# A third residual tile, nine exponential rooms, two banks by turns for the values' sums, and ten pairs of heads a tile in the first FFN blocks

## The chip, the core and the metric

The kernel runs on one core of a Trainium2 chip. The core has a matrix engine (TensorE, PE in the profile, with its weight loads as PEld), a vector engine (VectorE, DVE), an engine for functions (ScalarE, ACT), a general engine (GpSimd, POOL) and a queue that issues transfers (SyncE, SP). Each runs its own instructions in the order of the program and waits for the others by semaphores. Matrix products land in PSUM, eight banks of 128 x 512 numbers of four bytes; all else lies in the on-chip memory SBUF. The metric is the device time of one execution in microseconds (us), lower is better.

## What is computed

One transformer layer on 2048 tokens of 576 features, everything in 32-bit floats: layer norm, attention of 32 query heads of 18 features over one shared key and value head, a residual, a second layer norm, and a bilinear FFN with 4608 hidden features and a residual.

```python
def _A_ref(x, wq, wk, wv, wo):
    q = (x @ wq).reshape(B, S, H, Dh).transpose(0, 2, 1, 3)
    k, v = x @ wk, x @ wv
    scores = jnp.einsum("bhqd,bkd->bhqk", q, k) * (Dh ** -0.5)
    p = _softmax(scores, axis=-1)
    o = jnp.einsum("bhqk,bkd->bhqd", p, v)
    return o.transpose(0, 2, 1, 3).reshape(B, S, H * Dh) @ wo
...
h = x + _A_ref(_layernorm(x), A_wq, A_wk, A_wv, A_wo)
g, u = _layernorm(h) @ w_gate, _layernorm(h) @ w_up
return h + (g * u) @ w_down
```

## The kernel before

**Blocks, groups and pairs.** The tokens fall into four blocks of 512 queries. Attention of a block is eight groups of four heads; a group goes over sixteen stretches of 128 keys, and for each stretch there are two pairs of heads. So `pair` (line 576) is called 256 times a block, 1024 times in all, in one fixed order counted by `n_pair`. One call issues the scores: two products that run at the same time in two halves of the array, into a PSUM room of two banks (`ps_s`, two rooms), and one exponential on ScalarE of 128 x 1024 numbers from that room into an SBUF room P (`p_tile`, line 566; six rooms at first, seven from the 240th pair). The pair is half of a stretch (`half`); when the second is issued the stretch is put into `pend`. `flush(n)` (line 604) takes the n oldest stretches of `pend` and issues their values: eight matrix instructions for each stretch, which sum P times V over the keys of a group in one PSUM bank (`ps_a`), the four heads in four strips of 32 columns. At a group's last stretch DVE turns the sum (`os`, line 612), and the rest of the group's work is put into the list `aux`: dividing by the row sums (`normalise`), every two groups splitting a chunk of heads in a high and a low part (`chunk`), multiplying it with the output weights and adding to the residual (`project`), and after the fifth chunk the statistics of the second layer norm. `run_aux` (line 621) takes one or two due entries at a time.

**The FFN.** `ffn(b)` (line 970) goes over 36 tiles of 128 hidden features for the 512 tokens of block b. A tile has 27 steps j, nine pieces of the features times three combinations of high and low parts; a step is two products side by side, one for the gate (`pg`) and one for the up half (`pu`). While there are pairs of the blocks up to b + 2 left (`on`), the tile issues a pair before steps 0, 4, 8, 12, 16, 20, 24 and one behind the copy of the gate: eight, except in the last tile of a block but the fourth, which issues none. Then ScalarE copies `pg` (`g`, line 1020), DVE multiplies `pu` with it into the hidden tile (`hf`, line 1024), and all stretches in `pend` are flushed. Without pairs left, `pg` and `pu` share one of the rooms that the scores had (`gu`). Hidden tiles come in couples, an even and an odd one. Their sums and splits (`left_first` in the odd tile, `left`, `left_sums` in the next even tile behind step 8, a cast of 128 x 1024 numbers on ScalarE) make the left side of a down product, which `down` (line 896) issues at the end of the next even tile: fourteen stages of three products of 128 x 288 in three banks, two of `ps_f` and one of `ps_m`. After a stage the partial sum is added to the residual, either by DVE or by a copy on ScalarE (`tmp`, a ring of five) and an addition on POOL. A stage that returns to a bank waits for the reader of the stage before it.

**PSUM.** Two rooms of two banks for scores, two banks `f` (for `pg`, `pu`, y), one bank `m` (y, and small products), one bank `a` (the values' sum): eight in all.

**Weights and residuals.** `load_w` (line 850) brings the FFN weights of a tile (576 KB) into one of two rooms `wr`; `split_w`, behind step 3, splits the next tile's weights on POOL and DVE into one of two rooms `ws` and then asks for the load two tiles ahead. `split_wo_0` (line 722) splits the five pieces of the first block's output weights; three rooms `wo_r` hold them as they come, and a fourth and a fifth piece are asked for behind the splits of the second and third. The residual of a block is a tile `h` of 512 tokens; there are two. The third block's is loaded at the end of `ffn(0)` (line 1041), into the room that the first block's output leaves, the fourth's at the end of `ffn(1)`. `project` of a block runs only when its residual is there (`b in self.h`, line 681).

**Order.** `run` (line 1160) first does keys, values and queries beside the first pairs, then `blocks` (line 1120), which finishes attention of the first block, and then the four `ffn`. The program order on every engine is written out by these calls.

Of the kernel before, what the change touches and what calls it, by code (L numbers as in the profile page):

```python
# [25 lines left out]
P = 128  # L26
# [28 lines left out]
class Block:  # L55
# [20 lines left out]
    def ps_m(self, name):  # L76
        return self.ps.tile([P, TB], F32, tag="m", bufs=1, name=name)
# [4 lines left out]
    def ps_a(self, name):  # L82
        return self.ps.tile([P, TB], F32, tag="a", bufs=1, name=name)
# [520 lines left out]
    def flush(self, n):  # L604

        for b, g, t, Ps in self.pend[:n]:
            if t == 0:
                self.acc = self.ps_a(f"acc{b}_{g}")
            self.values(self.acc, Ps, t)
            if t == NT - 1:  # L610
                os_ = self.os[g] = self.op.tile([P, TB], F32, tag="os", bufs=1, name=f"os{b}_{g}")
                self.dve.transpose(os_, self.acc)
                if b == 0 and g == NG - 1:
                    self.normalise(b, g, os_)
                else:
                    self.aux.insert(len(self.aux) if b else 0, (self.round + 1, lambda b=b, g=g, o=os_: self.normalise(b, g, o), None))
        del self.pend[:n]
# [80 lines left out]
    def chunk_of(self, b, c):  # L698
        to = self.heads_to(b, c)
        (self.split_tail if b and c == 4 else self.split)(*to, self.ob[0:rows(b, c), c])  # L700

# [15 lines left out]
    def load_wo_0(self, c):  # L717

        r = self.wo_r0[c] = self.w0.tile([P, D], F32, tag="wo_r", bufs=3, name=f"wo_r{c}")
        self.sp.dma_start(r, self.wo0[:, c])  # L720

    def split_wo_0(self):

        self.wo_0 = self.wp.tile([P, 2, 5, D], F32R, tag="X", bufs=1, name="wo_0")
        for c in range(3):
# [124 lines left out]
    def load_w(self, n):  # L850

        if n < NF * NB:
            r = self.wr[n] = self.wp.tile([P, 9, P], F32, tag="wr", bufs=2, name=f"wr{n}")
            self.sp.dma_start(r, self.wgu[n % NF])

    def split_w(self, n):
        if n < NF * NB:
# [3 lines left out]
            self.load_w(n + 2)  # L861
# [34 lines left out]
    def down(self, b, pair):  # L896
# [4 lines left out]
        if pair == NC - 1:  # L901
# [13 lines left out]
            def add(s, n):  # L915
                hs, y = h[:, s, n * HD:(n + 1) * HD], ys.pop((s, n))[:, :HD]
                if b < NB - 1 and n:
                    z = self.tmp[:, self.n_tmp % 5]
# [27 lines left out]
        for i, (t, bank, (x, w), first, (s, n), on_dve) in enumerate(STAGES):  # L946
# [7 lines left out]
            else:  # L954
                z = self.tmp[:, self.n_tmp % 5]
# [5 lines left out]
    def room(self):  # L961
# [5 lines left out]
        self.tmp = self.hh.tile([P, 5, HD], F32, tag="tmp", bufs=1, name="tmp")  # L967
        self.n_tmp = 0

    def ffn(self, b):  # L970
        pe, act, dve = self.pe, self.act, self.dve
        X, hid, todo = self.X, [], None
        for f in range(NF):
# [56 lines left out]
            if todo and on:  # L1030
                drain(self.down(b, *todo))
                self.more_wd(b, 7)
# [12 lines left out]
    def load_x(self, b):  # L1045
        h = self.h[b] = self.hp.tile([P, NQ, D], F32, tag="h", name=f"h{b}")
# [64 lines left out]
    def begin(self, first):  # L1111
# [6 lines left out]
        self.p_next, self.wo_r0, self.wo_in, self.yos, self.n_yo, self.due, self.odd = -1, {}, set(), [], 0, 0.0, 0  # L1118

    def blocks(self):  # L1120
# [4 lines left out]
        self.load_w(1)  # L1125
# [28 lines left out]
        else:  # L1154
            self.load_wd(WD_BUFS)
        for b in range(NB):
# [3 lines left out]
    def run(self):  # L1160
# [6 lines left out]
        self.tqs, self.p2 = [], None  # L1167
        self.begin(True)
        with ExitStack() as st:
# [3 lines left out]
            self.ps, self.w0 = pool("ps", 1, space=PSUM), pool("w0", 3)  # L1173
# [7 lines left out]
            with tc.tile_pool(name="p0q", bufs=1) as self.p0q:  # L1181
# [4 lines left out]
                with tc.tile_pool(name="qb", bufs=2) as self.qb:  # L1186
# [7 lines left out]
                    while live:  # L1194
                        if self.n_pair >= WO_FROM and not self.wo_r0:
                            for c in range(3):
# [10 lines left out]
            self.wp, self.hh, self.p2 = pool("w", 2), pool("hid", 4), pool("P2", 1)  # L1207
# [17 lines left out]
P2_FROM = 240  # L1225
# [126 lines left out]
```

## Time and profile before

| what | us |
|---|---|
| median of three runs | 2287.75 |
| lowest and highest run | 2286.09, 2287.89 |
| profiled execution, first to last instruction (span) | 2285.5 |
| mean of one exponential (1024 of them) | 1.027 |
| mean of one copy of y (408) | 0.400 |
| mean of one cast of the sums S (68) | 1.043 |
| mean of one multiplication hf (96 with pairs) | 0.691 |

The profile tells the span of the profiled execution, from its first to its last instruction; it gives no other time for it. The span lies 0.6 us below the lowest of the runs. In the chain of waits a row is a start in us, a duration in us, an engine with what it writes and the line, and how often. In a timeline the duration is that of the merged instructions from the first start to the last end; the brackets give the idle time of the engine before them and what ended it. In a group of instructions the numbers behind the bar are the busy time in us, the mean of one in ns, and the idle time before them in us with what ended most of it. PEld is the loading of weights into the matrix engine, which may run beside its products.

### The profile page before, as it was taken

The numbers are of one execution on the slowest core, as the hardware profiler recorded it, in microseconds if no ns is written. First come the engines' busy times: TensorE is split into PE (matmuls) and PEld (weight loads), VectorE is DVE, ScalarE is ACT, GpSimd is POOL, SyncE is SP. The second block draws the span as 40 slices with busy tenths as digits, with TensorE's granted clock in tenths as the row PEclk, the third lists the DMA queues.
The fourth block names the chain that finished last, engine by engine and source line by source line (L and its number), as shares of the span: only waits on it lengthen the run. The fifth ranks groups of instructions, "written<-read, shape, count | busy, mean of one in ns | idle before, by whom it ended". The sixth has DMA issues, their size and how long they took to land.

```text
span 2285.5 us, 45923 instructions
## 1 busy us (share of the span) xinstructions
PE 2264.4 (99%) x18114; PEld 1610.0 (70%) x18114; DVE 1183.9 (52%) x2152; ACT 1438.0 (63%) x1877; POOL 683.1 (30%) x856
## 2 busy tenths in 40 slices
PE   8999999999999999999999999999999999999998
PEld 6433345677777667677767777777767788898887
DVE  8332435565656566343434455444444476566565
ACT  5899887777676676767666767667677623232332
POOL 4000002455554444122221222222122233333332
PEclk9999999999999999999999999999999999999999
DMA  5222314444333444633333443643333355655553
GB/s 174 75 79 72 117 30 136 144 143 147 134 123 129 141 159 135 210 114 123 113 113 108 126 129 125 193 126 120 100 120 116 122 172 174 212 172 172 179 185 112
DMA packets 127129, 306.75 MB, mean 134 GB/s; under 512 B 17553, under 2 KB 17681, under 8 KB 126265
## 3 DMA queue, kind: packets, MB, share of 16 engines
q1 hardware_dynamic: 126905, 303.73, 40.6%
q8 instruction: 145, 2.38, 0.4%
q14 instruction: 79, 0.65, 0.1%
HBM read 233.76 MB, written 55.67 MB: 127 GB/s over the span
## 4 chain that ended last, share of the span: by engine, by line
PE 95%; DVE 2%; DMA 1%; ACT 1%; issue 0%; SPq 0%; POOL 0%; DVEq 0%; ACTq 0%; POOLq 0%
PE pg L990 21%; PE acc L601 20%; PE y L950 17%; PE gu L990 13%; PE s L596 12%; PE pu L990 5%; PE yo L754 3%; PE psq L448 2%; PE y L908 1%; DMA X<-X 1%; PE psk L236 0%; DVE XT L89 0%; PE ye L908 0%; DVE bsa L103 0%; ACT P L597 0%
## 5 line engine op out<-in xcount | busy, mean ns | idle before, releaser
L597 ACT ACTIVATE P<-s 128x1024 f32<-128x1024 f32 x1024 | 1025.4, 1027 | 263.6 <-PE s L596 187.1
L990 PE MATMUL pg<-X,ws 64*128 64x512 f32 x2592 | 702.6, 389 | 0.1
L990 PE MATMUL pu<-X,ws 64*128 64x512 f32 x2592 | 702.5, 389 | 0.1
L990 PEld LDWEIGHTS pg<-X,ws 64*128 64x128 f32 x2592 | 479.4, 185 | 69.2 <-issue 1.2
L990 PEld LDWEIGHTS pu<-X,ws 64*128 64x128 f32 x2592 | 477.3, 185 | 15.2 <-DVE h L755 1.0
L601 PE MATMUL acc<-P,V 128*32 128x512 f32 x4096 | 487.9, 598 | 0.0
L596 PE MATMUL s<-q,kT 56*128 56x512 f32 x2048 | 452.6, 421 | 3.6 <-DVE XT L89 1.8
L950 PEld LDWEIGHTS y<-wdo,room 128*128 128x128 f32 x2856 | 386.1, 188 | 47.6 <-issue 44.2
L950 PE MATMUL y<-wdo,room 128*128 128x288 f32 x2856 | 403.6, 300 | 0.1
L957 ACT COPY tmp<-y 128x288 f32<-128x288 f32 x408 | 162.9, 400 | 331.0 <-PE y L950 313.5
L596 PEld LDWEIGHTS s<-q,kT 56*128 56x128 f32 x2048 | 210.4, 184 | 188.7 <-ACT P L597 106.9
L990 PE MATMUL gu<-X,ws 64*128 64x512 f32 x2592 | 301.7, 389 | 0.6 <-DMA X<-X 0.6
L958 POOL TENSOR_TENSOR x<-x,tmp 128x288 f32<-128x288 f32 x204 | 159.1, 808 | 440.7 <-ACT tmp L957 439.8
L601 PEld LDWEIGHTS acc<-P,V 128*32 128x32 f32 x4096 | 113.9, 109 | 241.6 <-issue 230.6
L990 PEld LDWEIGHTS gu<-X,ws 64*128 64x128 f32 x2592 | 250.1, 184 | 46.3 <-issue 4.7
L88 POOL CAST ws<-wr 128x1152 fp32r<-128x1152 f32 x144 | 171.4, 1190 | 321.8 <-PE pu L990 173.5
L958 POOL TENSOR_TENSOR h<-h,tmp 128x288 f32<-128x288 f32 x204 | 159.0, 810 | 345.4 <-ACT tmp L957 345.1
L89 DVE TENSOR_TENSOR ws<-wr,ws 128x1152 fp32r<-128x1152 f32 x144 | 199.8, 1387 | 75.4 <-POOL ws L88 75.4
L1024 DVE TENSOR_TENSOR hf<-pu,g 128x512 f32<-128x512 f32 x96 | 66.3, 691 | 265.3 <-ACT g L1020 258.6
L953 DVE TENSOR_TENSOR x<-x,y 128x288 f32<-128x288 f32 x272 | 117.4, 453 | 145.5 <-PE y L950 145.5
L953 DVE TENSOR_TENSOR h<-h,y 128x288 f32<-128x288 f32 x272 | 118.1, 454 | 112.0 <-PE y L950 108.9
L89 DVE TENSOR_TENSOR room<-S,room 128x1024 fp32r<-128x1024 f32 x68 | 85.5, 1257 | 144.3 <-ACT room L88 144.3
(172 smaller groups left out, 1630.2 us busy)
## 6 DMA issues: line engine op xcount, KB each, us to landing
wdo<-wd_dram SPq DMA_DIRECT2D x369, 288.0 KB
wr<-in_wgu_dram SPq DMA_DIRECT2D x144, 576.0 KB
wd_dram<-wdo SPq DMA_DIRECT2D x123, 288.0 KB
q<-q_dram SPq DMA_DIRECT2D x64, 216.0 KB
raw<-in_wd_dram SPq DMA_DIRECT2D x36, 288.0 KB
q_dram<-qs SPq DMA_DIRECT2D x15, 504.0 KB
X<-X SPq DMA_DIRECT2D x24, 256.0 KB
ob<-ob SPq DMA_DIRECT2D x121, 36.0 KB
```

The source lines that it names most:

```text
L88: (copy or self.cast)(hi, src)
L89: self.dve.tensor_tensor(lo, src, f32(hi), ALU.subtract)
L596: self.pe.matmul(s_[:, i], self.kT[o:o + 56, t * P:(t + 1) * P], q[o:o + 56, pr], start=True, stop=True)
L597: self.act.activation(p_, s_, AF.Exp, scale=SCALE)
L601: self.pe.matmul(acc[32 * j:32 * j + 32, :], self.V[:, t, :], Ps[j // 2][:, j % 2, :], start=(t == 0), stop=(t == NT - 1), skip_group_chec ...
L754: pe.matmul(y[:, :HD], m, k, start=(i == 0), stop=(i == len(ms) - 1))
L950: pe.matmul(y[:, :HD], m[:, t * P:(t + 1) * P], k, start=(first and j == 0), stop=(j == 2), skip_group_check=True)
L953: dve.tensor_tensor(hs, hs, y[:, :HD], ALU.add)
L957: act.copy(z, y[:, :HD])
L958: pool.tensor_tensor(hs, hs, z, ALU.add)
L990: pe.matmul(ps, w[o:o + 64, wk, c], X[o:o + 64, xk, c], start=(j == 0), stop=(j == 26))
L1024: dve.tensor_tensor(hf, pu, g, ALU.mult)
```

## The change

Six things change together.

- **Pairs.** `SPOTS` replaces the seven spots: two pairs before step 0 and one before steps 5, 9, 13, 16, 20 and 24, and as before one behind the copy of the gate: nine a tile. In tiles that issue a down product, one or two more are issued behind the flush and ahead of the product, so many that no half stretch is left over. The last tile of a block only completes a half stretch.
- **Values' sums.** From the second block on each group takes the other of the banks `a` and `m` (`acc_at`), and `ps_m` hands out the one that is not in use for the sum.
- **Rooms P.** Nine once the first output weights are split: six as before, two (`early`) that hold those weights before, and one more (`late`). The output weights come through two rooms instead of three.
- **FFN weights.** One room `wr` instead of two; the load is asked for one tile ahead.
- **Residuals.** The third block has a tile of its own (`h2`), loaded ahead of the FFN; the fourth block's is loaded at the end of `ffn(0)`.
- **Order.** The first group of the third and fourth block is normalised only when the block before has split its last chunk (`split_to`).

```diff
     def ps_m(self, name):
-        return self.ps.tile([P, TB], F32, tag="m", bufs=1, name=name)
+        return self.ps.tile([P, TB], F32, tag="am"[self.acc_at == 0], bufs=1, name=name)
...
     def ps_a(self, name):
-        return self.ps.tile([P, TB], F32, tag="a", bufs=1, name=name)
+        return self.ps.tile([P, TB], F32, tag="am"[self.acc_at], bufs=1, name=name)
...
-        i = self.p_next = (self.p_next + 1) % (P_BUFS + (self.p2 is not None and self.n_pair >= P2_FROM))
-        pool, tag = (self.pp, "P") if i < P_BUFS else (self.p2, "P2")
+        i = self.p_next = (self.p_next + 1) % (P_BUFS + (EARLY + LATE if len(self.wo_in) == 5 else 0))
+        pool, tag = (self.pp, "P") if i < P_BUFS else (self.early, "P2") if i < P_BUFS + EARLY else (self.late, "P3")
...
             if t == 0:
+                if b:
+                    self.acc_at = 1 - self.acc_at
                 self.acc = self.ps_a(f"acc{b}_{g}")
...
-                    self.aux.insert(len(self.aux) if b else 0, (self.round + 1, lambda b=b, g=g, o=os_: self.normalise(b, g, o), None))
+                    free = (lambda b=b: self.split_to >= b) if g == 0 and b > 1 else None
+                    self.aux.insert(len(self.aux) if b else 0, (self.round + 1, lambda b=b, g=g, o=os_: self.normalise(b, g, o), free))
...
-        r = self.wo_r0[c] = self.w0.tile([P, D], F32, tag="wo_r", bufs=3, name=f"wo_r{c}")
+        r = self.wo_r0[c] = self.early.tile([P, D], F32, tag="P2", name=f"wo_r{c}")
...
-            if 0 < c < 3:
-                self.load_wo_0(c + 2)
+            if c + EARLY < 5:
+                self.load_wo_0(c + EARLY)
...
-            r = self.wr[n] = self.wp.tile([P, 9, P], F32, tag="wr", bufs=2, name=f"wr{n}")
+            r = self.wr[n] = self.wp.tile([P, 9, P], F32, tag="wr", bufs=1, name=f"wr{n}")
...
-            self.load_w(n + 2)
+            self.load_w(n + 1)
...
-                    if on and not last and j % 4 == 0 and self.more(b + 2):
-                        self.pair()
+                    if on:
+                        for _ in range((j == 0 and len(self.half)) if last else SPOTS.count(j)):
+                            if self.more(b + 2):
+                                self.pair()
...
             self.flush(len(self.pend))
             if todo and on:
+                for _ in range(0 if last else 2 - len(self.half)):
+                    if self.more(b + 2):
+                        self.pair()
                 drain(self.down(b, *todo))
...
-            if b + 2 < NB:
-                self.load_x(b + 2)
+            if b == 0:
+                self.load_x(3)
...
     def load_x(self, b):
-        h = self.h[b] = self.hp.tile([P, NQ, D], F32, tag="h", name=f"h{b}")
+        pool, tag = (self.hp2, "h2") if b == 2 else (self.hp, "h")
+        h = self.h[b] = pool.tile([P, NQ, D], F32, tag=tag, name=f"h{b}")
...
         self.load_w(0)
-        self.load_w(1)
...
+        self.load_x(2)
         for b in range(NB):
             self.ffn(b)
...
-P2_FROM = 240
+EARLY, LATE = 2, 1
+N_TMP = 5
+SPOTS = (0, 0, 5, 9, 13, 16, 20, 24)
```

More of the change, by code (lines that the diff above doesn't have):

```diff
@@ L724, in split_wo_0 @@
         self.wo_0 = self.wp.tile([P, 2, 5, D], F32R, tag="X", bufs=1, name="wo_0")
-        for c in range(3):
+        for c in range(EARLY):
             if c not in self.wo_r0:
@@ L917, in add @@
                 if b < NB - 1 and n:
-                    z = self.tmp[:, self.n_tmp % 5]
+                    z = self.tmp[:, self.n_tmp % N_TMP]
                     self.n_tmp += 1
@@ L954, in down @@
             else:
-                z = self.tmp[:, self.n_tmp % 5]
+                z = self.tmp[:, self.n_tmp % N_TMP]
                 self.n_tmp += 1
@@ L966, in room @@
         self.S = self.hh.tile([P, 4, HT], F32, tag="S", bufs=1, name="S")
-        self.tmp = self.hh.tile([P, 5, HD], F32, tag="tmp", bufs=1, name="tmp")
+        self.tmp = self.hh.tile([P, N_TMP, HD], F32, tag="tmp", bufs=1, name="tmp")
         self.n_tmp = 0
@@ L1172, in run @@
             self.qp, self.pp, self.op, self.otp = pool("q", 2), pool("P", P_BUFS), pool("o", 1), pool("oT", 1)
-            self.ps, self.w0 = pool("ps", 1, space=PSUM), pool("w0", 3)
+            self.ps, self.early = pool("ps", 1, space=PSUM), pool("P2", EARLY)
             self.C = cp.tile([P, C_W], F32, name="C")
```

10 lines of the change are left out of this document (6 added, 4 removed).

## The prediction

> **What bounds the kernel now.** The page comes first.
>
> ```profile
> span 2285.5 us, 45923 instructions
> PE 2264.4 (99%) x18114; PEld 1610.0 (70%) x18114; DVE 1183.9 (52%) x2152; ACT 1438.0 (63%) x1877; POOL 683.1 (30%) x856
> ...
> PEclk9999999999999999999999999999999999999999
> ...
> PE 95%; DVE 2%; DMA 1%; ACT 1%; issue 0%; SPq 0%; POOL 0%; DVEq 0%; ACTq 0%; POOLq 0%
> ```
>
> TensorE (PE) is busy all the time at the full clock, and 95% of the chain that ended last is its own work. ScalarE (ACT) is busy 63% of the span, on the mean. As a busy PE is a modelled number, I next read the chain of waits in order of time, to see whether PE streams without gaps: two tiles of the first FFN block (a left one closes each), then two tiles late in the last.
>
> ```profile
> 422.90 3.57 PE acc L601 x32
> 426.47 5.84 PE y L950 x42
> ...
> 456.04 5.84 PE y L950 x42
> ...
> 1985.07 5.84 PE y L950 x42
> 1990.92 12.46 PE gu L990 x108
> 2003.38 5.83 PE y L950 x42
> ```
>
> From one down product to the next are 456.04 - 426.47 = 29.57 us with sixteen pairs, and 2003.38 - 1985.07 = 18.31 us without. The second is 12.46 + 5.84: nothing but streaming. In the first, sixteen pairs cost 11.26 us, 0.70 each. A pair's own work is one step of scores (0.23 us below) and 3.57/8 = 0.45 us of values, 0.68; 16 x 0.68 = 10.82 leaves 0.44 us over for a two-tile round, 0.22 a tile, spent where PE goes from one kind of product to another. So **PE streams now, and the change removes no product**: it can win the 0.22 us of a tile that loses its pairs, and lose wherever PE is made to wait.
>
> **The part that gains.** The groups by line say how many tiles carry pairs.
>
> ```profile
> L1024 DVE TENSOR_TENSOR hf<-pu,g 128x512 f32<-128x512 f32 x96 | 66.3, 691 | 265.3 <-ACT g L1020 258.6
> ...
> L1024 DVE TENSOR_TENSOR hf<-gu,g 128x512 f32<-128x512 f32 x48 | 33.0, 687 | 78.2 <-ACT g L1020 78.2
> ```
>
> 96 tiles have pairs, 48 have none. Two of the 96 are last tiles of a block and issue none, so they hold 94 x 8 = 752 of the 1024 pairs; 272 come before the FFN. By the new code tiles 0 and 1 of a block issue 9 each, tile 2 issues 10, then odd ones 9 and even ones 11, and the last none: 348 a block. Two blocks take 696, and 56 are left: six tiles of the third. So 78 tiles carry pairs, 18 fewer: 18 x 0.22 = **-4.0 us**.
>
> **The part that costs: scores meet ScalarE.** The scores have two PSUM rooms (each two banks); the scores of a pair wait until the exponential of two pairs before has read its room. I read ACT and then PE in one even tile, the one that ends with the 426.47 product.
>
> ```profile
> 415.08 3.32 ACT L597 ACTIVATE P<-s 128x1024 f32<-128x1024 f32 x3 [1.48 <-PE s L596]
> 418.30 1.04 ACT L88 CAST room<-S 128x1024 fp32r<-128x1024 f32 x1
> 419.23 3.87 ACT L597 ACTIVATE P<-s 128x1024 f32<-128x1024 f32 x4
> 423.00 0.58 ACT L1020 COPY g<-pg 128x512 f32<-128x512 f32 x1
> 423.99 1.02 ACT L597 ACTIVATE P<-s 128x1024 f32<-128x1024 f32 x1 [0.41 <-PE acc L601]
> 427.95 0.40 ACT L957 COPY tmp<-y 128x288 f32<-128x288 f32 x1 [2.93 <-PE y L950]
> ```
>
> ```profile
> 414.48 0.50 PE L596 MATMUL s<-q,kT 56*128 56x512 f32 x2
> ```
>
> ```profile
> 419.18 0.39 PE L596 MATMUL s<-q,kT 56*128 56x512 f32 x2
> 419.41 0.39 PE L990 MATMUL pg<-X,ws 64*128 64x512 f32 x1
> ...
> 420.32 0.50 PE L596 MATMUL s<-q,kT 56*128 56x512 f32 x2
> 420.66 0.39 PE L990 MATMUL pg<-X,ws 64*128 64x512 f32 x1
> ...
> 422.51 0.39 PE L596 MATMUL s<-q,kT 56*128 56x512 f32 x2
> 422.83 1.06 PE L601 MATMUL acc<-P,V 128*32 128x512 f32 x8
> ...
> 426.40 2.41 PE L950 MATMUL y<-wdo,room 128*128 128x288 f32 x16
> ```
>
> ```profile
> 420.31 0.18 PEld L596 LDWEIGHTS s<-q,kT 56*128 56x128 f32 x2 [0.26 <-ACT P L597]
> ```
>
> A step of PE is 0.23 us (419.18 to 419.41), five steps to a spot now. A full exponential lasts 1.03; as the first two of the four span 1.94 us,
>
> ```profile
> 419.23 1.94 ACT L597 ACTIVATE P<-s 128x1024 f32<-128x1024 f32 x2
> ```
>
> the next starts 1.94 - 1.03 = 0.91 behind; 0.92 is taken. The cast of S holds ACT for 419.23 - 418.30 = 0.93. The scores at 420.32 just reach their room: the cast has pushed the fourth exponential to 419.23, it ends at 420.26, and the weight load follows at 420.31. No time is waited, but the load wasn't done ahead, and the step takes 0.34 instead of 0.23: 0.11 us lost. **The present spacing of four is exactly used up by the cast.**
>
> Now the new spots 0, 0, 5, 9, 13, 16, 20, 24, with zero at the tile's first scores. The first scores' load finds values before it, so the step is 0.34: second scores at 0.34, first product at 0.57; the scores of spot 5 at 0.57 + 5 x 0.23 = 1.72. Exponentials: 0.60 (415.08 - 414.48), 1.52, 2.44; the cast, which still stands behind the third, at 3.36; the fourth at 4.29, ending at 5.32. The scores of spot 5 need the first, over at 1.63: in time, but with no load ahead, 0.1 lost. Spot 9 comes at 1.72 + 0.34 + 4 x 0.23 = 2.98, spot 13 at 4.13, spot 16 only four steps later at 5.05. It needs the fourth exponential, free at 5.32 + 0.05 = 5.37: a **wait of 0.32 us, and 0.11 for the load**. Spots 20, 24 and the last then find their rooms open. Together 0.53 against 0.11 now, +0.42 us. Even tiles with a cast are 17 in each of two blocks and two in the third, 36: **+15 us**. Bounds: from 0 (ACT's sum of 7 x 0.92 + 0.93 = 7.4 us fits into the 7.5 us from the first exponential to the last scores, so a better order would hide it) to 0.8, if lags add up at spot 20 too.
>
> In odd tiles a shorter cast, of half a hidden tile, stands there. The same layout keeps every room open; spot 5 is short of its early load: 0.05 us x 36 = +2 us (0 to 0.15 each).
>
> **Two pairs ahead of the down product.** They are scores between values and y. Values to y is a change of kind now; afterwards it is values to scores and scores to y. The nearest row is scores to values, 422.51 to 422.83, 0.32 instead of 0.23: +0.09. Their exponentials also come in front of the copies of y on ACT's queue: the two scores start 0.65 us before y, the exponentials at -0.05 and +0.87, so the first copy starts at +1.79 and not at 427.95 - 426.40 = +1.55. It ends at +2.19, and the sixth stage of the product, which adds on to that bank, is due after five stages of 0.41, at +2.1: a wait of 0.14 with the lag, and about 0.06 for a load not ahead. Queued behind that copy are the other five; they have gaps between them and catch up. 0.29 x 36 = **+10 us** (0 to 0.45 each).
>
> **Costed at little.** Rooms: the row at 423.99 has the last exponential wait for values now, with seven rooms. Nine rooms serve ten pairs and the one held over; in odd tiles the exponential of spot 24 waits for the first values, about 1.2 us behind their start, and the copy of g behind it. Hidden by the rest of the values (five times 0.89 us): hf is done some 3.5 us into 4.5. Without that cover it would cost an us a tile. Two banks by turns: a group of 32 pairs now ends within a flush; the other bank lets the next group's values go on while DVE turns the old sum, and only a y in the old bank could wait, a few times in all: 0. Two rooms for the first output weights, by these rows:
>
> ```profile
> 278.39 1.51 SPq L720 DMA_DIRECT2D wo_r<-in_wo_dram  x2
> ```
>
> ```profile
> 284.77 1.99 POOL L88 CAST wo<-wo_r 128x576 fp32r<-128x576 f32 x2 [5.88 <-DMA wo_r<-in_wo_dram]
> ```
>
> ```profile
> 281.20 0.75 DVE L89 TENSOR_TENSOR wo<-wo_r,wo 128x576 fp32r<-128x576 f32 x1
> ```
>
> The third piece, split at 281.20, will be asked for only at 278.39. The fourth, asked for then, took 6.4 us behind two FFN weights; with one of these ahead I take 4. Split and DVE's adds behind it come some 1.5 us late, PE has three y banks before it feels that: +1 (0 to +4). A chunk's split on ACT (self.cast) may fall into a full tile, ten in two blocks at 0.1: +1 (0 to +4). The third residual tile is an earlier load beside the first blocks: 0.
>
> **Sum.** -4 + 15 + 2 + 10 + 1 + 1 = +25 us on the span of 2285.5, which lies 2.3 us below the median of 2287.75: **2313 us**, 1.1% slower. All lower ends give 2284, all upper ones 36 x (0.8 + 0.15 + 0.45) = 50, and 8 - 4: 2342.
>
> **The rivals.** *The waits don't show.* If ACT's order or PE's queue takes the 0.3 us up, what is left is the 18 tiles: 2287.75 - 4 = 2284. For it: ACT has time, 20 x 0.92 + 0.93 + 2 x 0.6 + 6 x 0.4 = 23 us and two shorter casts in a new round of some 33. Against it: the row at 420.31 shows the margin used up already. It is on the side of faster from the point where a round waits less than 4/36 = 0.11 us in all. *Half of it*: the down product's copies catch up but the cast doesn't, or the reverse: 2293 to 2300. *The single room for FFN weights.* The load of a weight now starts only when the split of the one before is over, and in tiles without pairs a round of 18.31 us has two of them.
>
> ```profile
> L88 POOL CAST ws<-wr 128x1152 fp32r<-128x1152 f32 x144 | 171.4, 1190 | 321.8 <-PE pu L990 173.5 <-PE gu L990 105.7 <-PE pg L990 30.8
> ```
>
> Now the cast waits for PE alone: for the products of two tiles before, in at least 310 of the 321.8 us, and no load is among the three named. The longer way from one split to the next but one's start, a tile and a down product, is 6.23 + 5.84 = 12.1 us; less 1.2 for the cast and about as much for DVE's half, a load has some 10 us (an estimate from these rows). Each us beyond that is lost once in a round, 33 rounds: a load of 11 us gives 2313 + 33 = 2346, from 10 us on it is slower than the forecast. The row at 284.77 (6.4 us) speaks against it, seven loads of y weights in each round for it. The Trainium skill (Trainium Kernel Development and Optimization, Best Practices) says to double-buffer so that loads hide behind compute, which speaks against this part; its DMA: Bandwidth & Descriptors (Anatomy of one DMA) fits 2.0 us plus bytes over 436 kB a us, as an estimate 3.4 us for 576 KB, by which the single room would hold and the sum stays. No row of before shows such a load alone. *That the change doesn't do what it says*: if chunks or residuals held the pairs back, ScalarE would still be busy late in the third block, and the 4 us would not be won.
>
> **A rule weighed.** The row at 420.31 shows a weight load that waited for its room, and 0.11 us lost behind it. The Trainium skill (TensorE: Matmul & The Clock Gate, Architectural detail) has PE's queue pull weight loads ahead of matmuls in flight, while ScalarE keeps strict order. Taken as if such a load were always hidden, the losses at spot 5 (0.1 and 0.05) and at y (0.06) go, 36 x 0.21 = 8 us, and the sum is +17, 2305; by the row it stays +25. On ScalarE's order rows and rule agree.
>
> **How the numbers follow.** Forecast (both waits, 2300 to 2328): 0.58. Half of it (2290 to 2300): 0.14. The waits don't show (2280 to 2289): 0.18. The single room late (above 2328): 0.07. The change held back (2286 to 2292, nothing won or lost): 0.03. A measurement here tells 0.2%, 4.6 us, from no change: faster is below 2283.2, same up to 2292.3. Of the third case half lies below, 0.09, and 0.02 for gains I don't see: faster 0.11; same 0.09 + 0.03 + a fifth of the half case, 0.15; slower 0.74. The range leaves out the third case's lower half and what is above 2328: 2284 to 2328.
>
> **What would show it.** Right: in even tiles of the first block the weight load of the fifth spot's scores (spot 16) follows the end of the fourth exponential by 0.05 us, and PE's step there is 0.4 us longer; a round of 20 pairs takes 29.57 + 4 x 0.68 + 0.84 = 33.1 us; 78 tiles have pu; the first copy of y starts 0.2 us later behind the first y. Wrong: a round of 32.3 us (the waits don't show); rounds without pairs above 18.31 us with POOL's cast waiting for wr (the single room); pairs in more than six tiles of the third block. The forecast falls with the cast of S: if ACT takes it elsewhere than behind the third exponential, the 15 us go.

## The result, and the profile after

| what | before | after |
|---|---|---|
| median of four runs each, us | 2286.93 | 2324.44 |
| lowest and highest run, us | 2286.09, 2287.89 | 2322.08, 2325.56 |
| span of the profiled execution, us | 2285.5 | 2322.9 |

The changed kernel is slower by a ratio of 1.0161 (95% interval 1.0147 to 1.0176). The forecast of 2313 us had the side right and was 11 us short. The first lines of the page after, and its chain by engine:

```profile
span 2322.9 us, 45901 instructions
...
PE 2285.7 (98%) x18114; PEld 1589.5 (68%) x18114; DVE 1202.2 (52%) x2152; ACT 1410.1 (61%) x1877; POOL 684.9 (29%) x856
...
PE 79%; ACT 7%; DVE 6%; issue 4%; DMA 3%; SPq 1%; POOL 0%; ACTq 0%; DVEq 0%; POOLq 0%
```

The number of PE's instructions is the one of before, 18114; its busy time grew by 21 us all the same, so part of its waiting is counted as busy. The chain says it better: PE's own share fell from 95% to 79%, and 7% of ACT, 6% of DVE and 3% of DMA stand in it now. The chain in order of time shows where. First two rounds of the first block (a round is the time from one down product to the next, two tiles), then a place in the last block, where no pairs are left:

```profile
433.31 6.03 PE y L955 x42
...
466.40 6.03 PE y L955 x42
...
2091.40 5.82 PE y L955 x42
2097.22 6.37 PE gu L997 x54
...
2111.24 4.69 PE y L955 x33
```

With pairs a round is 466.40 - 433.31 = 33.09 us; 33.1 was forecast. The down product takes 6.03 us instead of 5.84. Without pairs, the chain no longer runs on PE alone: a product of 42 appears as its last 33, since the chain leaves PE behind the ninth for whoever released it. Over sixteen rounds of the last block the median is 18.60 us; before, it was 18.31.

The groups by line:

```profile
L1031 DVE TENSOR_TENSOR hf<-pu,g 128x512 f32<-128x512 f32 x78 | 54.0, 692 | 273.6 <-ACT g L1027 273.6
...
L88 POOL CAST ws<-wr 128x1152 fp32r<-128x1152 f32 x144 | 170.9, 1187 | 376.7 <-DMA wr<-in_wgu_dram 211.0 <-PE pu L997 158.2 <-PE gu L997 7.3
```

78 tiles have `pu`, as worked out (two of them are last tiles of a block and issue no pair, so the table below counts 76). But POOL's cast of the FFN weights, which waited for PE alone before, now waits 211 us for the load.

To see how the 37 us are made up, I took from each tile's time what its products need when PE streams (per product 0.114 us for FFN and scores, 0.111 for values, 0.137 for y: the steps between neighbours of one kind in the trace). What is left is time lost on PE:

| lost on PE, us | before | forecast | after |
|---|---|---|---|
| ahead of the first FFN tile | 78.3 | 79.3 | 78.9 |
| tiles with pairs (94, then 76) | 44.2 | 66.3 | 65.4 |
| tiles without (50, then 68) | 16.9 | 18.8 | 32.6 |

The forecast column is the column of before with the prediction's own terms: 18 tiles change sides (0.325 lost in a tile with pairs, 0.105 without), and +28 for the waits in tiles with pairs. **The tiles with pairs came out as forecast, within 1 us. The whole error lies in the tiles without pairs: 14 us that I had costed at nothing.**

### The profile page after: what moved, and what is told of

Same layout as the page of the kernel before. It is cut to its first block, busy times and chain, and to the rows that moved or that the text cites. A ratio compares the mean times of both kernels' runs of the same rounds, so it can differ in the third digit from the quotient of the medians.

```text
span 2322.9 us, 45901 instructions
## 1 busy us (share of the span) xinstructions
PE 2285.7 (98%) x18114; PEld 1589.5 (68%) x18114; DVE 1202.2 (52%) x2152; ACT 1410.1 (61%) x1877; POOL 684.9 (29%) x856
## 4 chain that ended last, share of the span: by engine, by line
PE 79%; ACT 7%; DVE 6%; issue 4%; DMA 3%; SPq 1%; POOL 0%; ACTq 0%; DVEq 0%; POOLq 0%
PE acc L601 19%; PE y L955 16%; PE gu L997 13%; PE pg L997 12%; PE s L596 11%; ACT P L597 5%; PE yo L759 3%; PE pu L997 3%; PE psq L448 2%; DVE ws L89 1%; ACT room L88 1%; DVE hf L1031 1%; DVE S L892 1%; PE y L913 1%; DMA ob<-ob 1%
## 5 line engine op out<-in xcount | busy, mean ns | idle before, releaser
L597 ACT ACTIVATE P<-s 128x1024 f32<-128x1024 f32 x1024 | 1000.9, 1030 | 340.9 <-PE s L596 248.3
L997 PE MATMUL pu<-X,ws 64*128 64x512 f32 x2106 | 571.6, 390 | 0.4 <-DVE hf L1031 0.4
L997 PE MATMUL pg<-X,ws 64*128 64x512 f32 x2106 | 570.4, 389 | 0.0
L596 PE MATMUL s<-q,kT 56*128 56x512 f32 x2048 | 428.3, 426 | 11.5 <-ACT P L597 9.5
L997 PEld LDWEIGHTS pg<-X,ws 64*128 64x128 f32 x2106 | 389.9, 185 | 69.0 <-issue 1.2
L997 PE MATMUL gu<-X,ws 64*128 64x512 f32 x3564 | 417.0, 390 | 1.8 <-POOL ws L88 1.0
L997 PEld LDWEIGHTS pu<-X,ws 64*128 64x128 f32 x2106 | 389.1, 185 | 5.6 <-DVE hf L1031 0.8
L997 PEld LDWEIGHTS gu<-X,ws 64*128 64x128 f32 x3564 | 341.9, 185 | 68.7 <-issue 6.2
L596 PEld LDWEIGHTS s<-q,kT 56*128 56x128 f32 x2048 | 192.0, 184 | 229.6 <-ACT P L597 132.4
L1027 ACT COPY g<-gu 128x512 f32<-128x512 f32 x66 | 38.9, 589 | 161.7 <-PE gu L997 161.7
```

The costliest lines, as they stand in the source:

```text
L596: self.pe.matmul(s_[:, i], self.kT[o:o + 56, t * P:(t + 1) * P], q[o:o + 56, pr], start=True, stop=True)
L597: self.act.activation(p_, s_, AF.Exp, scale=SCALE)
L997: pe.matmul(ps, w[o:o + 64, wk, c], X[o:o + 64, xk, c], start=(j == 0), stop=(j == 26))
```

## The experiments

**One: is the fifth spot's wait where the prediction put it?** The trace of the change answers by itself. ACT, PE and the weight loads of one even tile, which starts at 452.21 (timelines):

```profile
452.81 2.86 ACT L597 ACTIVATE P<-s 128x1024 f32<-128x1024 f32 x3 [0.99 <-PE s L596]
455.54 1.06 ACT L88 CAST room<-S 128x1024 fp32r<-128x1024 f32 x1
456.48 5.04 ACT L597 ACTIVATE P<-s 128x1024 f32<-128x1024 f32 x5
...
466.27 1.94 ACT L597 ACTIVATE P<-s 128x1024 f32<-128x1024 f32 x2 [2.84 <-PE s L596]
468.10 0.41 ACT L962 COPY tmp<-y 128x288 f32<-128x288 f32 x1
```

```profile
453.93 0.46 PE L596 MATMUL s<-q,kT 56*128 56x512 f32 x2
454.23 0.40 PE L997 MATMUL pg<-X,ws 64*128 64x512 f32 x1
...
457.01 0.39 PE L997 MATMUL pg<-X,ws 64*128 64x512 f32 x1
...
457.58 0.50 PE L596 MATMUL s<-q,kT 56*128 56x512 f32 x2 [0.18 <-ACT P L597]
457.91 0.40 PE L997 MATMUL pg<-X,ws 64*128 64x512 f32 x1
...
466.33 6.10 PE L955 MATMUL y<-wdo,room 128*128 128x288 f32 x42
```

```profile
457.58 0.19 PEld L596 LDWEIGHTS s<-q,kT 56*128 56x128 f32 x2 [0.61 <-ACT P L597]
```

Spot 5 is 1.72 us into the tile (forecast 1.72), spot 16 is 5.37 (forecast 5.37). The cast of S stands behind the third exponential; the fourth starts at 456.48 and ends near 457.51; the weight load, which had stood idle 0.61 us for it, follows at 457.58. The sizes can be read from PE's starts, where a full step is 0.23 us. The step ahead of these scores is 457.58 - 457.01 = 0.57, a wait of 0.34 (forecast 0.32); the step behind them is 457.91 - 457.58 = 0.33, where the load was not ahead, 0.10 more than a full one (0.11); the step at spot 5 is 454.23 - 453.93 = 0.30, 0.07 more (0.1). Over 31 even tiles the medians are 0.34, 0.11 and 0.07. Also as forecast: the two exponentials ahead of y start 0.06 us before it, and the first copy of y comes 468.10 - 466.33 = 1.77 us behind y's start (1.79).

Four edits then take these waits away, whole or in part. The later cast:

```diff
-                    if j == (8 if on else 2) and todo and not plain(n_ - 2):
+                    if j == (24 if on else 2) and todo and not plain(n_ - 2):
                         self.left_sums()
```

> The changed kernel with the split of the sums S issued behind step 24 instead of step 8 in tiles with pairs, so that ScalarE's cast of 1.04 us stands behind the exponential of spot 24. Theory (the cast pushes the fourth exponential, and spot 16's scores wait): the wait of 0.18 us and the late load at the fifth spot go, a round of twenty pairs takes 32.65 instead of 33.1 us, 36 rounds, 2308 to 2312 us. Rival (the loss in tiles with pairs is paid for changes between kinds of products, or ScalarE's queue just waits at another place): a round of 33.0 to 33.1 us, 2322 to 2326 us.

Measured: 2307.43 us (2304.92 to 2313.61), 17.0 below the change; a round with pairs is 32.63 (median). ACT in an even tile of this run:

```profile
450.82 8.24 ACT L597 ACTIVATE P<-s 128x1024 f32<-128x1024 f32 x8 [1.00 <-PE s L596]
458.96 1.04 ACT L88 CAST room<-S 128x1024 fp32r<-128x1024 f32 x1
```

Eight exponentials now run without a break and the cast comes behind them. 33.1 - 32.63 = 0.47 a round, over 36 rounds 17 us: the wait of 0.34, the late load of 0.11, and 0.02 more behind them. The loss at spot 5 stays.

The spot moved by one step instead:

```diff
-SPOTS = (0, 0, 5, 9, 13, 16, 20, 24)
+SPOTS = (0, 0, 5, 9, 13, 17, 20, 24)
```

> The changed kernel with spot 17 instead of spot 16, nothing else. By the layout the scores come one step of 0.23 us later to a room that opens at 5.37 us in the tile, so that 0.23 of the 0.32 us of wait goes: rounds of twenty pairs of 32.85 to 32.9 instead of 33.1 us, 36 rounds, 7 to 9 us less, 2315 to 2318 us. Rival (the cast's place alone decides, as the late cast took 0.47 us, and the wait only moves to the next spot): rounds of 33.05 to 33.1 us, 2322 to 2326 us.

Measured: 2316.78 (2314.43 to 2319.0), 7.7 below; rounds 32.89. One step of 0.23 us takes back 0.2 us of the round, as expected: the wait is where it was said to be.

No pairs ahead of the down product:

```diff
-                for _ in range(0 if last else 2 - len(self.half)):
+                for _ in range(0):
```

> The changed kernel without the pairs ahead of the down product: nine pairs a tile, some 84 tiles with pairs. Theory (their exponentials push the first copy of y, 0.2 us, and a change of kind, 0.09): the down product is back at 5.84 us, a round of eighteen pairs takes 31.4 us; 36 x 0.29 = 10 us won, 3 lost in six more tiles with pairs and two more casts: 2316 to 2319 us. Rival (only the change of kind costs): 2322 to 2326 us.

Measured: 2317.42 (2312.46 to 2319.4), 7.0 below. A round, now of 18 pairs, is 31.37. Its chain:

```profile
428.26 5.84 PE y L955 x42
...
459.61 5.84 PE y L955 x42
```

The product is at 5.84 again, as before. Without those two pairs a round of 20 would be 31.37 + 2 x 0.68 = 32.73; the two pairs ahead of the product cost the rest, 33.1 - 32.73 = 0.37. That 84 tiles instead of 76 issue pairs now (beside two last tiles, with one pair each) gives a part of it back.

The prediction put 0.14 us of this on the sixth stage of the product, which waits for ScalarE's late first copy (the reader of the third stage). Here DVE adds the third stage instead:

```diff
-STAGES = [..., (0, 2, P5, True, (1, 1), False),
+STAGES = [..., (0, 2, P5, True, (1, 1), True),
```

> The changed kernel with the third stage of the down product added by VectorE instead of copied by ScalarE, so that the copy behind the two exponentials is not waited for. Theory (the down product takes 6.03 instead of 5.84 us since the first copy comes late): it takes 5.84 to 5.9 us, rounds of 32.9 us, 5 to 7 us less, 2317 to 2320 us. Rival (the 0.19 us are the changes of kind, or VectorE is late at the same place): 6.0 us, 2322 to 2326 us.

Measured: the product is back at 5.84 and a round at 32.97, 0.14 less; the mechanism holds. But the time is 2323.23 (2319.28 to 2324.47), hardly less than the change's. A few irregular tiles became longer (in the profile, one in the third block by 3.0 us, two in the first by 2.0 and 1.1). Why, I did not find out. The one of 2.0 us, the third tile, is longer by 2.3 us in the trace of a later run too (ScalarE's cast of the weights, below), whose edit does not touch tiles with pairs. So the total of this run decides nothing.

**Two: where do the 14 us in tiles without pairs come from?** The suspect is the single room `wr`, my rival of 0.07. First it alone, put into the kernel before:

```diff
-            r = self.wr[n] = self.wp.tile([P, 9, P], F32, tag="wr", bufs=2, name=f"wr{n}")
+            r = self.wr[n] = self.wp.tile([P, 9, P], F32, tag="wr", bufs=1, name=f"wr{n}")
...
-            self.load_w(n + 2)
+            self.load_w(n + 1)
...
-        self.load_w(1)
```

> The kernel before with one FFN weight room instead of two, and nothing else of the change. Theory (the single room is what makes tiles without pairs longer): rounds without pairs go from 18.31 us to 18.5 to 18.9, POOL's cast waits for the load of wr, rounds with sixteen pairs stay at 29.6; with 48 tiles without pairs that is 8 to 14 us, 2295 to 2301 us. Rival (something else that moved into those tiles makes them longer: residual loads, output stores, the order of the rest of a group): no change, 2285 to 2290 us, and no wait for wr.

Measured: 2297.04 (2294.73 to 2297.64), ratio 1.0047 (1.0030 to 1.0064). Rounds without pairs are 18.57, rounds with pairs 29.59, as before (29.60, medians). The reverse, the change with its two rooms back (and four `tmp` copies of y in place of five, to make place):

```diff
-            r = self.wr[n] = self.wp.tile([P, 9, P], F32, tag="wr", bufs=1, name=f"wr{n}")
+            r = self.wr[n] = self.wp.tile([P, 9, P], F32, tag="wr", bufs=2, name=f"wr{n}")
...
-            self.load_w(n + 1)
+            self.load_w(n + 2)
...
+        self.load_w(1)
...
-N_TMP = 5
+N_TMP = 4
```

> The changed kernel with two FFN weight rooms again; the ring of copies of y has four places instead of five to make room for it. Theory: rounds without pairs return to 18.3 us, 12 to 16 us less than the changed kernel, 2308 to 2313 us; rounds with twenty pairs stay at 33.1. Rival (another cause in those tiles): 2322 to 2326 us.

Measured: 2307.83 (2306.64 to 2310.15), 16.6 below the change; rounds without pairs 18.31, with pairs 33.11 as in the change. So the single room costs 10 us in the kernel before, with 50 tiles without pairs, and 17 in the change, with 68.

How it costs them is not what I had written. I had said that a load has 10 us; in the last block of the change a load is asked for at 2100.63 and POOL's cast of it starts 4.0 us later. SP, POOL, DVE and PE around it (timelines):

```profile
2100.63 10.55 SPq L859 DMA_DIRECT2D wr<-in_wgu_dram  x2
```

```profile
2104.65 1.15 POOL L88 CAST ws<-wr 128x1152 fp32r<-128x1152 f32 x1 [5.44 <-DMA wr<-in_wgu_dram]
```

```profile
2105.01 1.06 DVE L892 TENSOR_TENSOR S<-hf,hf 128x256 f32<-128x256 f32 x1
...
2108.32 1.23 DVE L89 TENSOR_TENSOR room<-S,room 128x1024 fp32r<-128x1024 f32 x1 [0.52 <-ACT room L88]
2109.47 1.35 DVE L89 TENSOR_TENSOR ws<-wr,ws 128x1152 fp32r<-128x1152 f32 x1
2110.73 0.81 DVE L958 TENSOR_TENSOR h<-h,y 128x288 f32<-128x288 f32 x2
```

```profile
2109.61 1.45 PE L955 MATMUL y<-wdo,room 128*128 128x288 f32 x9
2111.24 1.05 PE L955 MATMUL y<-wdo,room 128*128 128x288 f32 x6 [0.17 <-DVE h L958]
```

The same work in the kernel before, POOL and DVE:

```profile
2052.23 1.15 POOL L88 CAST ws<-wr 128x1152 fp32r<-128x1152 f32 x1 [4.44 <-PE gu L990]
```

```profile
2053.60 0.42 DVE L887 TENSOR_TENSOR S<-hf,hf 128x256 f32<-128x256 f32 x1
...
2057.41 1.35 DVE L89 TENSOR_TENSOR ws<-wr,ws 128x1152 fp32r<-128x1152 f32 x1
2058.91 0.85 DVE L953 TENSOR_TENSOR h<-h,y 128x288 f32<-128x288 f32 x2
```

Before, POOL's cast is over (2053.38) when DVE begins the first sum of S, which takes 0.42 us. After, the cast begins a little ahead of that sum, and the sum takes 1.06. DVE's chain from there to the first addition of y has little slack: seven instructions, with a wait for ACT's cast in between, whose end at 2057.41 + 1.35 = 2058.76 lies only 0.15 us ahead of the addition in the kernel before; and the addition frees the bank that the fourth stage of the down product needs. So PE stops behind the ninth product.

In the last block's 17 such sums none takes over 0.6 us in the kernel before, 13 do after. In all fifteen where the cast had begun first, the sum ends 0.272 to 0.275 us behind the cast's end, however long that is. In the one that began first (by 0.07 us), the sum takes 0.43 and the cast 1.37 instead of 1.15. One of the two waits for the other to end: that is no sharing but a lock. It is what the Trainium skill says (SBUF — State Buffer, Who interferes with whom): a VectorE instruction with two SBUF inputs and a GpSimd instruction that reads SBUF use one port in common, and whoever issues first holds it to its end. These rows agree.

If that is the cause, it goes when another engine casts. ScalarE, in tiles without pairs:

```diff
-    def split_w(self, n):
+    def split_w(self, n, copy=None):
...
-            self.split(w[:, 0], w[:, 1], r, self.nc.gpsimd.tensor_copy)
+            self.split(w[:, 0], w[:, 1], r, copy or self.nc.gpsimd.tensor_copy)
...
-                        self.split_w(n_ + 1)
+                        self.split_w(n_ + 1, None if on else act.copy)
```

> The changed kernel, with one edit: in tiles without pairs the upper half of the gate and up weights (ws<-wr) is cast by ScalarE instead of POOL; there is still one room for the raw weights, and the load still lands as late as it did. Theory (POOL's late cast runs beside VectorE's first sum of S, which then takes 0.6 to 1.4 us in place of 0.42, and VectorE's chain up to the additions of y is late by that): no sum of the last block takes over 0.6 us, rounds without pairs fall from 18.6 towards 18.3, and about 8 to 14 us of 2324 go: 2310 to 2317 us. Rival (the late load itself holds VectorE up, whoever casts): rounds without pairs stay at 18.55 to 18.65 and the time at 2321 to 2327 us. Second rival (ScalarE's cast, now behind its cast of the room of S, sets the subtraction of ws back by more than the sum gains): rounds above 18.65, over 2327 us.

The same edit in the kernel before with one room:

> The kernel before with a single room for the raw gate and up weights (2297 us) and, in tiles without pairs, their cast on ScalarE instead of POOL. Theory (late cast beside VectorE's sum of S): the 10 us that the single room cost go for the most part: 2286 to 2290 us, rounds without pairs from 18.57 to 18.3. Rival (the late load itself): it stays at 2294 to 2299 us.

Measured: 2319.35 (2317.05 to 2320.72), 5.1 below the change, and 2292.98 (2291.76 to 2295.14), 4.1 below the run with one room alone. Rounds without pairs are 18.46 and 18.44, and both times lie between what the theory and its rival gave. The mean of the first sum over the whole kernel (groups by line, of before, after and the run with ScalarE's cast):

```profile
L887 DVE TENSOR_TENSOR S<-hf,hf 128x256 f32<-128x256 f32 x68 | 30.1, 442 | 2.3
```

```profile
L892 DVE TENSOR_TENSOR S<-hf,hf 128x256 f32<-128x256 f32 x68 | 41.5, 611 | 2.3
```

```profile
L892 DVE TENSOR_TENSOR S<-hf,hf 128x256 f32<-128x256 f32 x68 | 29.7, 436 | 2.3
```

The long sums are gone (none of the 17 in either run), and so is PE's stop behind the ninth product. In its place the product as a whole has become 0.15 us longer than in the kernel before:

```profile
2108.72 6.04 PE L955 MATMUL y<-wdo,room 128*128 128x288 f32 x42
```

In the same view of the kernel before:

```profile
2058.21 5.89 PE L950 MATMUL y<-wdo,room 128*128 128x288 f32 x42
```

In the trace with ScalarE's cast the surplus stands in the seventh and the eleventh stage, some 0.07 each. These stages wait for the third and the fourth addition of y on DVE, and each of the two begins 0.40 to 0.41 us behind its products' last start instead of 0.33. In front of them stands a wait instruction that neither the change nor the kernel before has there: in 16 of the last block's 17 down products both additions wait for POOL beside PE. The view by line counts these waits on DVE (the change, then ScalarE's cast):

```profile
L958 DVEq EVENT_SEMAPHORE  x136: 21/21/21, 404.8 to 2302.6; - x136
```

```profile
L958 DVEq EVENT_SEMAPHORE  x192: 21/21/21, 406.8 to 2299.0; - x192
```

The parts of the residual that the two additions write were last written by POOL, a round earlier. As long as POOL casts the weights, DVE waits for that cast anyway, and so for everything that POOL did ahead of it; without it each addition has to wait for POOL by itself, and pays 0.07 for a wait that ended long ago. That this is the reason is read from the program and the waits, not tried in a run of its own. So the lock is shown as the cause of the stop that the change has. Its removal by this edit brings half of the round's 0.29 us, since the edit adds two delays of 0.07 of its own. With two rooms nothing is late, and all of it goes.

A second part of the 17 us is at one place, the seam from the third block to the fourth. There SP issues the next activations, the output and y weights first, and the load of a weight comes behind them. Chain, POOL and PE of the change:

```profile
1976.17 6.29 DMA out_dram<-h
1982.53 6.18 DMA wr<-in_wgu_dram
```

```profile
1988.85 1.15 POOL L88 CAST ws<-wr 128x1152 fp32r<-128x1152 f32 x1 [10.71 <-DMA wr<-in_wgu_dram]
```

```profile
1990.06 0.73 PE L997 MATMUL gu<-X,ws 64*128 64x512 f32 x4 [0.97 <-POOL ws L88]
1991.45 7.56 PE L997 MATMUL gu<-X,ws 64*128 64x512 f32 x50 [0.66 <-DVE ws L89]
```

Here the load itself is late and PE waits for weights, as the rival had it: the second and third tile of the block with their product take 7.48 and 14.72 us, against 6.13 and 12.25 with two rooms, 3.8 us together.

**Three: do the parts add up, and is there a gain under them?** The later cast and two rooms together:

> The changed kernel with both repairs measured before, the late cast of S and two FFN weight rooms (four places in the ring of copies). If the two losses are separate, they add up: 2324 - 17 - 16 = 2291 us (2288 to 2295), rounds of 32.6 and 18.3 us. If one hides a part of the other (both act on ScalarE's or VectorE's order in the same tiles): 2296 to 2306 us.

Measured: 2292.7 (2290.58 to 2294.55), ratio 1.0025 (1.0015 to 1.0034); rounds 32.64 and 18.30. 17.0 + 16.6 = 33.6 were to go, 31.7 went: they add up within 2 us. Then also no pairs ahead of the down product:

> The kernel of the run before without the pairs ahead of the down product as well: nine pairs a tile, two weight rooms, the late cast. Theory: all three losses are gone, what is left is 84 instead of 96 tiles with pairs at 0.22 us, and the late cast's gain: 2280 to 2286 us, rounds of 30.9 us. Rival (a further cost of the change that no step names, in the first block above all): 2288 to 2295 us.

Measured: 2286.15 (2283.4 to 2288.95), ratio 0.9997 (0.9988 to 1.0006), just above what was expected. A round of 18 pairs is 30.91, which is 29.57 + 2 x 0.68 = 30.93: no cost is left over in the rounds as a whole (what the later cast takes from the old round, and what spot 5 adds, nearly cancel). But one tile of the first block loses 5.0 us. POOL there:

```profile
807.44 0.81 POOL L1088 TENSOR_TENSOR sums<-raw 128x288 f32<-128x288 f32 x1 [13.68 <-DMA raw<-in_wd_dram]
...
809.07 0.66 POOL L88 CAST wos<-wor 128x576 fp32r<-128x576 f32 x1
```

POOL stands 13.7 us for raw y weights, and the split of a piece of the next block's output weights is queued behind it. I gave that cast to ScalarE:

```diff
     def split_wo(self):
...
-            self.split(w[:, 0], w[:, 1], self.wo_r.pop(c), self.nc.gpsimd.tensor_copy)
+            self.split(w[:, 0], w[:, 1], self.wo_r.pop(c), self.act.copy)
```

> The kernel with two weight rooms, the late cast and no pairs ahead, with the output weights of the later blocks split by ScalarE instead of POOL. In the first block POOL waits 13.7 us there for the raw y weights, the split of the fourth piece stands behind, and one tile loses 5.0 us. Theory: that tile loses 0.5 to 1.5 us, 2281 to 2283 us, below both kernels. Rival (ScalarE's casts cost as much in other tiles, or the piece is late anyhow): 2285 to 2288 us.

Measured: 2281.75 (2279.13 to 2283.07), ratio 0.9976 (0.9967 to 0.9985); the tile loses 0.4 us now. This version (three residual tiles, nine rooms P, two banks by turns, nine pairs a tile, but a later cast, two weight rooms and no pairs ahead of the down product) beats both kernels, by 5.5 us (3.4 to 7.6) on the one before.

**Four: is the later cast a gain of itself?** If a load that isn't done ahead costs 0.11 us, as the prediction had read, the kernel before should gain from the later cast too:

> The kernel before with the split of S behind step 24 in tiles with pairs, and nothing else. Theory (the cast uses up the spacing of four, the load of one pair's scores is not done ahead, 0.11 us in each of some 45 rounds with pairs): rounds of 29.46 instead of 29.57 us, 5 us less, 2280 to 2283 us. Rival (the late load costs nothing, or the cast in its new place holds up the copy of g and the hidden tile): 2286 to 2290 us.

Measured: 2285.94 (2283.58 to 2287.65), ratio 0.9996 (0.9987 to 1.0005). ACT shows the cast behind seven exponentials, so that no load waits for the fourth, and PE shows what becomes of it (timelines):

```profile
414.94 7.90 ACT L597 ACTIVATE P<-s 128x1024 f32<-128x1024 f32 x7 [1.48 <-PE s L596]
422.74 1.03 ACT L88 CAST room<-S 128x1024 fp32r<-128x1024 f32 x1
...
424.15 1.04 ACT L597 ACTIVATE P<-s 128x1024 f32<-128x1024 f32 x1
```

```profile
414.34 0.50 PE L596 MATMUL s<-q,kT 56*128 56x512 f32 x2
...
422.57 3.73 PE L601 MATMUL acc<-P,V 128*32 128x512 f32 x32
426.22 0.66 PE L950 MATMUL y<-wdo,room 128*128 128x288 f32 x3
```

Regular rounds fell from 29.60 to 29.55 only (medians). But the late load was worth its 0.11. The values begin 422.57 - 414.34 = 8.23 us into the tile, 0.12 earlier than in the kernel before (422.83 - 414.48 = 8.35, by the prediction's lines). They then take 426.22 - 422.57 = 3.65 us up to y instead of 426.40 - 422.83 = 3.57, and give 0.08 of it back. The eighth exponential, which the cast and the copy of g now precede, ends 10.85 us into the tile instead of 10.53, and the values of its heads, in the last quarter of the 32 products, start 0.05 us behind that end. So the second half of the rival holds: the cast in its new place holds something up, though not the hidden tile but the last values. In the change, with 40 products of values instead of 32, the same edit loses nothing there (5.09 us from the first values to y with and without it).

## Why the prediction was right, and what it missed

- **Gain of 18 fewer tiles with pairs, -4.0.** The count is right, 78 tiles. The price of 0.22 us a tile was not measured alone: the version that is 5.5 us faster than the kernel before has 86 such tiles, ten fewer and not 18, which makes 2.2 us by that price. Where its other 3 us come from I did not take apart.
- **The cast of S pushes the fourth exponential, +15.** Right, in place (5.37 us into the tile) and in its parts: 0.34 for the wait (forecast 0.32), 0.11 for the load not done ahead (0.11), 0.07 at spot 5 (0.1), less the 0.11 that the kernel before lost already, 0.41 a round (0.42). The 17 us that the later cast brings are another sum: the 0.07 at spot 5 stays, and the late load of 0.11, which the kernel before had as well, goes too.
- **Odd tiles, +2.** Smaller: the step at spot 5 is 0.25 instead of 0.23 us (median of 34 odd tiles), 0.02 and not 0.05, so less than 1 us.
- **Two pairs ahead of the down product, +10.** Right: 0.37 a round against 0.29; the late first copy behind their exponentials is 0.14 of it, as forecast. Taking them away brought 7.0 us, as it also spreads the pairs over eight more tiles. The sign that the prediction gave, a round of 33.1 us, was added up wrongly: it adds 0.84, and the prediction's own terms make 0.42 + 0.05 + 0.29 = 0.76, a round of 33.05. Measured are 33.09.
- **First output weights +1, third residual, nine rooms and two banks 0.** Too small to tell: the first FFN tile begins at 360.5 instead of 359.8, but over the profiles of all runs this start lies anywhere from 358.2 to 361.8. The tiles with pairs show no cost beside those above.
- **The single weight room, 0 in the sum.** This is the step that failed: "a load has some 10 us", and below that nothing. That sum asked only whether the *next tile's products* would wait for the weights, and by it a load of 4.0 us is harmless. It did not ask what runs beside POOL's cast when the cast starts later. The cast now begins 4 us behind the load's issue, beside a sum of DVE that has to wait for its end: 0.29 us a round. The prediction's estimate of 3.4 us for such a load was near. The fit behind it the Trainium skill (DMA: Bandwidth & Descriptors, Anatomy of one DMA) gives for transfers that GpSimd issues, and these go by SP; no run here takes the two apart. Tile by tile against the profile with two rooms, which is 18.1 us shorter, the change loses 11 us in the light tiles of the third and fourth block, and 3.9 at the last block's seam, where the load stands behind others on SP. The other 3 us lie ahead of the FFN and in its third tile, and single runs vary there as much. With the 14 us of the tiles without pairs the sum is 2313 + 14 = 2327, against 2324.
- **The range.** The prediction had named this sign, rounds without pairs above 18.31 us and POOL's cast waiting for `wr`, at a chance of 0.07, for a load of more than 10 us. The sign came, but by another mechanism, and at the seam alone by the one it named. That the time still fell inside 2284 to 2328 is partly luck: the 15 us above the forecast were meant for larger waits in the tiles with pairs, and just held the 14 us that were missing.
- **The rule weighed**: by the Trainium skill (TensorE: Matmul & The Clock Gate, Architectural detail) a weight load is pulled ahead of the products, and the prediction priced that at 8 us less. The traces side with the row. A load whose room is open does start ahead of its product, by 0.23 us. One that has to wait for an exponential is not hidden: 0.11 us behind spot 16, where it starts with its product, and 0.07 and 0.02 at spot 5 in even and odd tiles, where it starts 0.04 and 0.08 ahead.

## What to carry to other kernels

When a buffer is taken away, asking whether its load still arrives in time is half of the question; the other half is beside which work the first instruction behind the load will now run, and whether the two share a port. On an engine that issues in order, place a long instruction (here a cast of 1 us on ScalarE) behind the last of a regular series, not inside it, when the series' spacing is used up, and then look at who needs the series' last member: in the change this brought 17 us, in the kernel before the last values gave most of it back. Look for a chain with little slack in the stages that have the least work, not only in the crowded ones: here the light tiles lost the 14 us that the forecast missed.

## What the runs showed of the hardware

- A sum of two SBUF operands on DVE (128 x 256, 0.42 us alone) that starts while POOL casts from SBUF ends 0.27 us behind the cast's end, in all 29 such overlaps in the last block of two traces (the change, and the kernel before with one room); begun first, it takes 0.43 and the cast 1.37 to 1.40 instead of 1.15.
- A load of 576 KB in the last block was followed by the cast that waits for it 4.0 us later (2100.63 to 2104.65); at the seam of the last block it took 6.3 us (1982.53 to 1988.85).
- A weight load of the scores that starts 0.23 us ahead of its product leaves a step of 0.23 us; 0.08 ahead 0.25, 0.04 ahead 0.30, and together with it 0.34 (medians in the change). Two pairs between values and y cost 0.37 us a round, 0.14 of it by ScalarE's late copy.
- An addition on DVE that also waits for POOL, whose work ended long before, started 0.07 us later behind the same products (32 of 34 in one trace).
